# Attention followed by a channel mix on one core: order of the first loads, one transfer per piece in the first two batches, and a new order of all steps

## The chip, the cores and the metric

The kernel runs on one core of a Trainium2 chip, in one launch. The metric is device time in microseconds (us); the median of three timed runs is 259.61 us. Five engines work from queues of their own, each strictly in the order in which the program put its instructions: TensorE (PE; its weight loads are listed apart as PEld), VectorE (DVE), ScalarE (ACT), GpSimd (POOL) and SyncE (SP, which here only starts transfers). Transfers to and from the main memory (DMA) are started from the queues of SP, ACT and POOL. PE writes its products into PSUM, from where DVE and ACT fetch them.

## The reference, cut to what matters

Eight batches, eight heads, 576 tokens, 64 values per head. Attention is causal by blocks of 64 tokens; its output, with the heads side by side, is the input `x` of a channel mix with a token shift.

```
def _attn_ref(q, k, v):
    scores = scale * np.matmul(q, k.transpose(0, 1, 3, 2))
    scores = np.where(mask, scores, -1000000000.0)      # block_i >= block_j
    attn = np.exp(scores - np.max(scores, axis=-1, keepdims=True))
    attn = attn / (np.sum(attn, axis=-1, keepdims=True) + 1e-09)
    return np.matmul(attn, v)

def _moe_ref(x, mu_k, mu_r, w_k, w_v, w_r):              # x: 8 x 576 x 512
    x_prev = np.concatenate([zeros, x[:, :-1, :]], axis=1)
    xk = mu_k * x + (1.0 - mu_k) * x_prev
    xr = mu_r * x + (1.0 - mu_r) * x_prev
    k = np.maximum(xk @ w_k, 0.0)                        # 512 -> 1024
    v = k * k @ w_v                                      # 1024 -> 512
    r = 1.0 / (1.0 + np.exp(-(xr @ w_r)))                # 512 -> 512
    return r * v
```

## The kernel before

The work is written as 678 steps (`plan.add`), each with an engine and a function that issues its instructions. The table `ORDER` gives the order in which they are issued, by number; a number with `+n` issues n unread products first, which write the identity times itself into a PSUM buffer that is overwritten afterwards (`unread`, L222). The string `PLACE` picks the engine of each step that may run on more than one. Waits follow from the data and from the rings of buffers (`RINGS`): four buffers `nb` for loaded queries and keys, two `lv` for loaded values, four PSUM buffers `ps`, ten for exponentials `e`. A buffer is given to the step that comes next in the order, so the order sets the waits too.

**Attention of a batch b.** Queries and keys come in four pieces (`qkld b g n`: g the group of heads, n = 1 for keys, 0 for queries), loaded from POOL's queue (L249) with a cast from four-byte to two-byte numbers. DVE turns each piece (`turn`, L260) into the layout that PE multiplies. In the batches of `HALVES`, 0 and 1, a group g holds two heads of each half of the heads, so that the first half of the score steps needs only the two pieces with g = 0; there a piece consists of two stretches of memory, and before the change each is a transfer of its own, to 64 partitions. Values come from SP and, for batch 0, also from ACT (`vld`, L284); one engine casts them (`vc`, L214), and small copies on ACT (`hold`, L293) keep the values of batch 0 back until the first piece of keys is there. Scores are PE products of one 64-token block against others (`sc b unit`, L365); ACT takes their exponential (`ex`, L386). PE then forms the sums of the exponentials (`sum`, L524, or `av b S`, L449) and the weighted values (`av`, L544 or L460). DVE turns the sums, inverts them and multiplies (`t1`, `rec`, `t2`, `norm`). Batch 0 goes in two parts of 256 and 320 tokens, the others whole: `av b S`, `T`, `A` and `B`, of 60, 16, 72 and 72 products.

**Channel mix.** `d` (POOL, DVE or ACT) and `mul` (DVE, L600 or L604) make the mixed inputs `xk` and `xr`. Over nine chunks of 512 tokens, PE forms `pk` (key weights WK, L644), `pr` (WR, L687) and `pv` (WV, L721); ACT or DVE takes the positive part (`relu`), one of three engines the square (`sq`), ACT the tanh (L697), DVE the final product (`o`, L731), and SP stores (L740). The weights are ten transfers from POOL's queue (`wld`, L324): four for WK, two for WR, four for WV. The mixing factors are four small transfers from SP (`mus`, L756), from which DVE makes tables (`mu1`, L762 to L766).

In this order POOL's queue begins with the four pieces of batch 0, a cast of values, WK, WR and then the pieces of batch 1; PE goes from the attention of batch 0 to `pr 0 0` and `pk 0 0 0` and only then to the scores of batch 1. PE's queue has 8118 rows, half of them weight loads. In the trace and here, "row" of PE means one instruction.

Of the kernel before, what the change touches and what calls it, by code (L numbers as in the profile page):

```python
# [12 lines left out]
ALU = mybir.AluOpType  # L13

ORDER = """
# [35 lines left out]
"""  # L51

PLACE = (
    "DDDDPDPAPADDAPPAADAADPPDDPAPDPAAPPDADAPPPDAADAPDDAPDPDPDPAADPAAAADPAAA"
    "AAAAADPDADPAADPAPAPAPDDDAADAADPDAAPAAAPADAPADAADPADAA")


class Plan:
# [8 lines left out]
    def add(self, key, alts, fn, deps=(), uses=(), **info):  # L67
        t = {"key": key, "alts": alts, "eng": alts[0], "fn": fn,
             "deps": [d for d in deps if d is not None],
             "uses": list(uses), "fill": 0, "info": info}  # L70
        for b in t["uses"]:
            b["left"] += 1
        self.tasks.append(t)
        return t
# [37 lines left out]
def kernel(  # L112
# [12 lines left out]
    nc = tc.nc  # L125
    B, H, S, D = q.shape
    C = H * D
    DF = moe_w_k.shape[1]
    P = 128
# [3 lines left out]
    GH = 4  # L133
    QC = P // GH
    JT = S // D
    RW = 32
    TOK = S // RW
# [21 lines left out]
    LW = TOK * D  # L159
# [13 lines left out]
    def new(buf):  # L173

        return slots[buf["ring"], buf["slot"]]

    identb = consts.tile([P, P], BF)
# [21 lines left out]
    HALVES = (0, 1)  # L199
    add = plan.add  # L200
# [17 lines left out]
    def unread(t, dst):  # L218


        for _ in range(t["fill"]):
            nc.tensor.matmul(  # L222
                dst, identb,
                identb[:, :].unsqueeze(1).to_broadcast([P, 4, P]),
                start=True, stop=True)
# [9 lines left out]
    def add_qk(b, g, n):  # L235

        src, qkt = (q, k)[n], qkt_buf[b]
        nb = plan.buf("nb")  # L240

        def rows():
            return new(nb)

        def fetch(eng, me):
            parts = ([(D * y, D, GH * y + 2 * g, 2) for y in range(2)]
                     if b in HALVES else [(0, P, GH * g, GH)])
            for p0, np_, h0, nh in parts:
                nc.gpsimd.dma_start(  # L249
                    rows()[p0:p0 + np_],  # L250
                    src[b, h0:h0 + nh].rearrange(
                        "y (r j) d -> (y r) (j d)", j=TOK))
        t = add(f"qkld {b} {g} {n}", ("POOL",), fetch, uses=[nb], kind="ldc",
                kb=P * LW * 4 / 1024, starts=2 if b in HALVES else 1)

        if n:
            loads.setdefault(b, (nb, t))

        def turn(eng, me):
            nc.vector.transpose(  # L260
                new(qkt)[:, n, g].rearrange("p t e -> p (t e)").bitcast(
                    FP).rearrange("p (r j) -> p j r", r=RW),
                rows()[:, :].bitcast(FP).rearrange(
                    "p (j s) -> p j s", s=RW))
        evac["qkt", b, g, n] = add(f"turn {b} {g} {n}", ("DVE",), turn, [t],
                                   uses=[nb, qkt], kind="turn", cols=S)
# [436 lines left out]
    def add_pv(c, j0):  # L703
# [42 lines left out]

    wbuf = plan.buf("ps")

    add("spare", ("PE",), lambda eng, me: unread(me, new(wbuf)[:, 0]), uses=[wbuf],
        kind="spare", cols=[])  # L750
    mu_ready = []

# [18 lines left out]
    for b in range(B):  # L771
        for g in range(2):
            for n in range(2):
                add_qk(b, g, n)
        for m in range(2):
            add_v(b, m)
        if b == 0:
            for name, n in (("k", 4), ("r", 2), ("v", 4)):
                for i in range(n):
                    add_w(name, i)  # L780
            for p, (lo, hi) in enumerate(PARTS):
                add_part(b, p, [add_unit(b, f"{p}{i}", pieces, b in SPLIT)
                                for i, pieces in enumerate(PIECES[p])])
                for cc in range(CCn):
                    add_mix(b, cc, lo, hi,
                            [ready["x", b, x, cc % 2]
                             for x in range(max(p - 1, 0), p + 1)])
        else:
            add_av(b, [add_unit(b, f"{i}", pieces, b in SPLIT)
                       for i, pieces in enumerate(WHOLE)])  # L790
            for cc in range(CCn):
                add_mix(b, cc, 0, S, [ready["x", b, "AB"[cc % 2]],
                                      ready["x", b, "T"]])
# [40 lines left out]
```

## Time and profile before

| what | value |
|---|---|
| timed runs | 259.23, 259.61, 263.8 us; median 259.61 |
| the profiled execution: its time | 262.33 us |
| the profiled execution: its span | 260.2 us |
| DVE, ACT, POOL busy | 188.8, 162.4, 80.3 us |
| main memory read and written | 33.56 MB and 9.44 MB |
| unread products | 38 |

The span runs from the first to the last instruction; the execution's own time holds 2.1 us more around it. Busy shares are averages over stages with different limits. In the lists of groups and in the timeline a row ends with the idle time of the engine just before it and what ended it; "issue" there means that the engine waited for nothing that the profile shows. In the views by stretch, each engine's busy time stands with its number of instructions in brackets, then PE's granted clock (1.00 is full), the busy share of the DMA engines (it can exceed 1, since packets overlap) and what they moved.

### The profile page before, as it was taken

The numbers are of one execution on the slowest core, as the hardware profiler recorded it, in microseconds if no ns is written. First come the engines' busy times: TensorE is split into PE (matmuls) and PEld (weight loads), VectorE is DVE, ScalarE is ACT, GpSimd is POOL, SyncE is SP. The second block draws the span as 40 slices with busy tenths as digits, with TensorE's granted clock in tenths as the row PEclk, the third lists the DMA queues.
The fourth block names the chain that finished last, engine by engine and source line by source line (L and its number), as shares of the span: only waits on it lengthen the run. The fifth ranks groups of instructions, "written<-read, shape, count | busy, mean of one in ns | idle before, by whom it ended". The sixth has DMA issues, their size and how long they took to land.

```text
span 260.2 us, 8926 instructions
## 1 busy us (share of the span) xinstructions
PE 242.6 (93%) x4058; PEld 132.3 (51%) x4058; DVE 188.8 (73%) x233; ACT 162.4 (62%) x184; POOL 80.3 (31%) x88
## 2 busy tenths in 40 slices
PE   8859498879999999999999999999999999999994
PEld 3536356654454446644454487444554764444442
DVE  1737889597888699899688969884699389444322
ACT  1456048877656969796777786786887743274220
POOL 6074256841405610060455234420000221142000
PEclk9988989997999999999999999999999999999999
DMA  5999996899699995449785930021002200300224
GB/s 88 194 165 189 207 217 103 134 191 215 102 253 238 168 208 181 90 96 215 196 137 97 215 110 3 3 98 65 4 5 81 83 5 12 150 3 0 81 82 161
DMA packets 49189, 31.50 MB, mean 121 GB/s; under 512 B 38528, under 2 KB 39808, under 8 KB 49152
## 3 DMA queue, kind: packets, MB, share of 16 engines
q1 hardware_dynamic: 40128, 18.29, 29.7%
q0 software_dynamic: 6688, 12.06, 27.6%
q10 hardware_dynamic: 2336, 0.59, 1.5%
q8 instruction: 31, 0.51, 0.8%
q14 instruction: 6, 0.05, 0.1%
HBM read 33.56 MB, written 9.44 MB: 165 GB/s over the span
## 4 chain that ended last, share of the span: by engine, by line
PE 84%; DMA 6%; ACT 3%; issue 3%; DVE 1%; POOL 0%; ACTq 0%; DVEq 0%; POOLq 0%
PE t_ps L644 25%; PE t_ps L721 23%; PE t_ps L687 12%; PE t_ps L365 10%; PE t_ps L460 8%; PE t_ps L449 4%; DMA t_lv<-in_v_dram 4%; ACT t_e L386 2%; PE t_ps L544 2%; DMA t_nb<-in_k_dram 1%; DMA out_dram<-t_o 1%; PE t_ps L222 1%; DVE t_o L731 1%; PE t_ps L524 1%; ACT L293 0%
## 5 line engine op out<-in xcount | busy, mean ns | idle before, releaser
L386 ACT ACTIVATE t_e<-t_ps 128x1024 f16<-128x1024 f32 (+4 forms) x98 | 87.6, 957 | 30.9 <-PE t_ps L365 30.1
L644 PE MATMUL t_ps<-t_xk,WK 128*128 128x512 f16 (+3 forms) x416 | 66.9, 314 | 0.4 <-ACT t_e L386 0.3
L721 PE MATMUL t_ps<-WV,t_k 128*128 128x512 f16 (+1 forms) x296 | 64.6, 374 | 0.0
L671 POOL TENSOR_TENSOR t_k<-t_kr 128x1024 f16<-128x1024 f32 x16 | 30.5, 1907 | 76.9 <-DVE t_kr L661 62.5
L644 PEld LDWEIGHTS <-WK 128*128 128x128 f16 x416 | 37.0, 98 | 26.1 <-issue 2.4
L721 PEld LDWEIGHTS <-t_k 128*128 128x128 f16 x296 | 28.1, 98 | 33.1 <-issue 1.9
L365 PE MATMUL t_ps<-t_qkt 32*64 32x64 bf16 (+7 forms) x1344 | 37.3, 290 | 6.1 <-ACT t_e L386 3.8
L260 DVE STREAM_TRANSPOSE t_qkt<-t_nb 128x576 f32<-128x576 f32 x32 | 38.1, 1242 | 1.5 <-PE t_ps L365 1.0
L697 ACT ACTIVATE t_t<-t_ps 128x1024 f32<-128x1024 f32 x18 | 18.5, 1028 | 31.5 <-PE t_ps L687 31.5
L687 PE MATMUL t_ps<-WR,t_xr 128*128 128x512 f16 x144 | 35.1, 390 | 0.4 <-ACT t_e L386 0.4
L659 ACT ACTIVATE t_kr<-t_ps 128x1024 f32<-128x1024 f32 x22 | 22.4, 1024 | 18.8 <-PE t_ps L644 18.3
L365 PEld LDWEIGHTS <-t_qkt 32*64 32x64 bf16 x1344 | 21.8, 106 | 22.9 <-issue 17.9
L731 DVE SCALAR_TENSOR_TENSOR t_o<-t_t,t_ps 128x1024 f32<-128x1024 f32 (+2 forms) x20 | 22.1, 1108 | 14.9 <-PE t_ps L721 9.9
L661 DVE TENSOR_SCALAR t_kr<-t_ps 128x1024 f32<-128x1024 f32 x14 | 17.1, 1224 | 19.5 <-PE t_ps L644 19.4
L584 POOL TENSOR_TENSOR t_d<-t_xt 128x576 f32<-128x576 f32 (+2 forms) x10 | 11.6, 1162 | 36.3 <-DVE t_xk L604 13.5
L687 PEld LDWEIGHTS <-t_xr 128*128 128x128 f16 x144 | 13.7, 100 | 17.2 <-issue 2.5
L460 PE MATMUL t_ps<-t_e,t_vo 64*32 64x512 f16 (+7 forms) x1120 | 21.6, 295 | 0.0
L460 PEld LDWEIGHTS <-t_vo 64*32 64x32 f16 x1120 | 14.9, 95 | 8.8 <-issue 4.5
L604 DVE SCALAR_TENSOR_TENSOR t_xk<-t_d,MU,t_xt 128x576 f16<-128x576 f32 (+2 forms) x24 | 19.2, 802 | 0.1
L497 DVE TENSOR_TENSOR t_xt<-t_ps,t_rt 128x1024 f32<-128x1024 f32 x14 | 16.9, 1218 | 3.2 <-PE t_ps L460 3.1
L580 ACT ACTIVATE t_d<-t_xt,MU 128x576 f32<-128x576 f32 (+1 forms) x24 | 16.8, 751 | 3.7 <-DVE t_xr L604 2.6
L214 POOL CAST t_vo<-t_lv 128x1152 f16<-128x1152 f32 x8 | 9.7, 1216 | 30.5 <-PE t_ps L460 19.3
(40 smaller groups left out, 181.7 us busy)
## 6 DMA issues: line engine op xcount, KB each, us to landing
out_dram<-t_o SPq DMA_DIRECT2D x17, 512.0 KB, 3.3
t_lv<-in_v_dram SPq DMA_DIRECT2D x30, 288.0 KB, 6.3
t_nb<-in_k_dram POOLq DMA_DIRECT2D x12, 288.0 KB, 6.4
t_nb<-in_q_dram POOLq DMA_DIRECT2D x12, 288.0 KB, 6.2
t_nb<-in_k_dram POOLq DMA_DIRECT2D x8, 144.0 KB, 6.3
t_nb<-in_q_dram POOLq DMA_DIRECT2D x8, 144.0 KB, 6.3
WK<-in_moe_w_k_dram POOLq DMA_DIRECT2D x4, 256.0 KB, 6.7
WV<-in_moe_w_v_dram POOLq DMA_DIRECT2D x4, 256.0 KB, 9.0
```

The source lines that it names most:

```text
L260: nc.vector.transpose(new(qkt)[:, n, g].rearrange("p t e -> p (t e)").bitcast(FP).rearrange("p (r j) -> p j r", r=RW), rows()[:, :].bitcas ...
L365: nc.tensor.matmul(new(ms[a // 2])[y * D:y * D + D, a % 2, col:col + n], qkt[rows, 1, g, t * D:t * D + D, f], qkt[rows, 0, g, q0:q0 + n, f ...
L386: nc.scalar.activation(new(e)[:, 2 * h:2 * h + 2, 0:w], new(ms[h])[:, :, 0:w], AF.Exp, scale=ISQ)
L460: nc.tensor.matmul(PA[o, u, HALF + f * D:HALF + f * D + D] if kind == "T" else PA[o, u, lo - D:lo - D + n], weight(b, u, c, t % JT, f), E[ ...
L604: e.scalar_tensor_tensor(dst, dt[:, 0, 0:W], MU1[:, n, cc % 2, cc // 2:cc // 2 + 1], x, ALU.mult, ALU.add)
L644: nc.tensor.matmul(ps[:, x, y * w + a:y * w + a + n], WK[:, cc, jc * P:(jc + 1) * P], MIX[0][:, cc, at:at + n], start=(cc == 0), stop=(cc ...
L659: nc.scalar.activation(kt, ps, AF.Relu, scale=ROOT)
L671: (nc.vector if eng == "DVE" else nc.gpsimd).tensor_tensor(dst, KR, KR, ALU.mult)
L687: nc.tensor.matmul(ps[:, x], MIX[1][:, cc, g:g + P], WR[:, cc], start=(cc == 0), stop=(cc == CCn - 1))
L697: nc.scalar.activation(new(tb), new(m), AF.Tanh, scale=0.5)
L721: nc.tensor.matmul(ps[:, x, cols], k2[:, jc, at:at + P], WV[:, jc, cols], start=(jc == 0), stop=(jc == JCn - 1))
L731: nc.vector.scalar_tensor_tensor(new(o)[:, xs, cols], new(tb)[:, xs, cols], 1.0, new(m)[:, xs, cols], ALU.add, ALU.mult)
```

## The change

Four things change.

1. `fetch` in `add_qk`: in batches 0 and 1 a piece is now one transfer to 128 partitions whose source is two stretches of 64 rows (`y` in the rearrangement), instead of two transfers to 64 partitions. The bytes are the same.
2. The first step, `spare`, issues 25 unread products instead of 27, and in two goes; with the new order there are 32 in all instead of 38.
3. `PLACE` gives other engines to the steps that have a choice: 16 `d` on ACT instead of 12, 9 on DVE instead of 14; 24 `relu` on ACT instead of 22; the second cast of batch 0's values on POOL instead of DVE, among others.
4. `ORDER` is new throughout. On POOL the pieces of batch 1 come ahead of the weights; on PE most score steps of batch 1 come between the attention steps of batch 0, ahead of `pr 0 0` and `pk 0 0 0`; on SP the mixing factors go behind the values; at the end `pr 8 0` goes two steps ahead of `pv 7 2 0`.

```
 ORDER = """
-1 0+27 5 3 9 2 7 11 6 15 12 16 13 17 4 29 33 56 30 10 60 34 64 57 68 8 61 72
...
+5 0+25 3 9 7 15 6 11 12 16 13 17 1 4 29 33 10 56 30 60 34 64 57 68 8 61 72 65
...
         def fetch(eng, me):
-            parts = ([(D * y, D, GH * y + 2 * g, 2) for y in range(2)]
-                     if b in HALVES else [(0, P, GH * g, GH)])
-            for p0, np_, h0, nh in parts:
+            if b in HALVES:
                 nc.gpsimd.dma_start(
-                    rows()[p0:p0 + np_],
-                    src[b, h0:h0 + nh].rearrange(
+                    rows(),
+                    src[b].rearrange("(y g h) (r j) d -> g y h r (j d)",
+                                     y=2, g=2, j=TOK)[g])
+            else:
+                nc.gpsimd.dma_start(
+                    rows(), src[b, GH * g:GH * g + GH].rearrange(
                         "y (r j) d -> (y r) (j d)", j=TOK))
...
-    add("spare", ("PE",), lambda eng, me: unread(me, new(wbuf)[:, 0]), uses=[wbuf],
+    SHORT = 0
+
+    def spare(eng, me):
+        dst, rest = new(wbuf)[:, 0], me["fill"]
+        me["fill"] = min(rest, 10)
+        unread(me, dst)
+        for n in range(SHORT):
+            at = n % GH * RW
+            nc.tensor.matmul(dst[at:at + RW, 0:D], identb[:, 0:RW],
+                             identb[:, 0:D], start=True, stop=True)
+        me["fill"] = max(rest - 10, 0)
+        unread(me, dst)
+    add("spare", ("PE",), spare, uses=[wbuf],
```

The loop over `SHORT` runs zero times.

**DVE, at the start of the program.** Before, DVE's queue after the constants; MUT and MU are the tables of mixing factors, t_nb the loaded pieces, t_qkt the turned ones.

```order
L196 MEMSET t_xt_125 128x4
L762 STREAM_TRANSPOSE MUT<-MUS 128x64
L764 TENSOR_SCALAR MU_156<-MUT 128x4
L766 TENSOR_SCALAR MU_157<-MUT 128x4
L762 STREAM_TRANSPOSE MUT<-MUS 128x64
L764 TENSOR_SCALAR MU_156<-MUT 128x4
L766 TENSOR_SCALAR MU_157<-MUT 128x4
L260 STREAM_TRANSPOSE t_qkt_111<-t_nb_107 128x18x32
```

Now, the same place.

```order
L196 MEMSET t_xt_125 128x4
L262 STREAM_TRANSPOSE t_qkt_111<-t_nb_107 128x18x32
L262 STREAM_TRANSPOSE t_qkt_111<-t_nb_108 128x18x32
L262 STREAM_TRANSPOSE t_qkt_111<-t_nb_109 128x18x32
L262 STREAM_TRANSPOSE t_qkt_111<-t_nb_110 128x18x32
L776 STREAM_TRANSPOSE MUT<-MUS 128x64
```

The tables moved behind the four turns of batch 0.

**POOL, behind the pieces of batch 0.** Before; t_lv are loaded values, t_vo cast ones, t_d and t_xt belong to the mix.

```order
L249 DMA t_nb_110<-in_q_dram 64x1152 x2
L214 CAST t_vo_113<-t_lv_105 128x1152
L324 DMA WK<-in_moe_w_k_dram 128x1024 x4
L324 DMA WR<-in_moe_w_r_dram 128x1024 x2
L249 DMA t_nb_107<-in_k_dram 64x1152 x2
L584 ISA
L584 TENSOR_TENSOR t_d_131<-t_xt_125 128x256
L249 DMA t_nb_108<-in_q_dram 64x1152 x2
```

Now, from the last piece of batch 0 to the first of batch 2.

```order
L247 DMA t_nb_110<-in_q_dram 128x1x1152
L214 CAST t_vo_113<-t_lv_106 128x1152
L247 DMA t_nb_107<-in_k_dram 128x1x1152
L247 DMA t_nb_108<-in_q_dram 128x1x1152
L214 CAST t_vo_113<-t_lv_105 128x1152
L247 DMA t_nb_109<-in_k_dram 128x1x1152
L247 DMA t_nb_110<-in_q_dram 128x1x1152
L326 DMA WK<-in_moe_w_k_dram 128x1024 x3
L586 ISA
L586 TENSOR_TENSOR t_d_130<-t_xt_125 128x256
L326 DMA WK<-in_moe_w_k_dram 128x1024
L586 TENSOR_TENSOR t_d_131<-t_xt_125 128x256
```

The four pieces of batch 1 now come ahead of all weights, one row each; a second cast and two subtractions stand between the transfers, and `WR` and the pieces of batch 2 follow below.

**ACT, behind the exponentials of batch 0.** Before; t_e are exponentials (t_e_121 the last of batch 0, t_e_122 the first of batch 1), t_t the tanh.

```order
L386 ACTIVATE t_e_121<-t_ps_143 128x2x320
L697 ACTIVATE t_t_138<-t_ps_143 128x1024
L580 ACTIVATE t_d_130<-t_xt_125,MU_157 128x320 x2
L386 ACTIVATE t_e_122<-t_ps_145 128x1024
L386 ACTIVATE t_e_123<-t_ps_144 128x1024
```

Now, the same place.

```order
L388 ACTIVATE t_e_121<-t_ps_142 128x2x320
L388 ACTIVATE t_e_122<-t_ps_144 128x1024
L388 ACTIVATE t_e_123<-t_ps_145 128x1024
L388 ACTIVATE t_e_124<-t_ps_142 128x1024
L582 ACTIVATE t_d_130<-t_xt_125,MU_157 128x256 x2
L388 ACTIVATE t_e_115<-t_ps_145 128x1024
```

The exponentials of batch 1 now follow those of batch 0 directly; the first tanh comes after eight of them.

More of the change, by code (lines that the diff above doesn't have):

```diff
@@ L15 @@
 ORDER = """
[35 rows of a table removed]
[35 rows of a table added]
 """
 PLACE = (
-    "DDDDPDPAPADDAPPAADAADPPDDPAPDPAAPPDADAPPPDAADAPDDAPDPDPDPAADPAAAADPAAA"
-    "AAAAADPDADPAADPAPAPAPDDDAADAADPDAAPAAAPADAPADAADPADAA")
+    "PPPAADPPDDAPAAPDPADPAPADDAAPPPAAPPDDPADAAADAPAAADAAAAAAAPDADDAPAAAPAPD"
+    "AAPDAAPAPAPAADDDDAPAADDDPDPAAADDPAAAAAPAADPDDAPAAAPAD")
 class Plan:
@@ L245, in fetch @@
         def fetch(eng, me):
-            parts = ([(D * y, D, GH * y + 2 * g, 2) for y in range(2)]
-                     if b in HALVES else [(0, P, GH * g, GH)])
-            for p0, np_, h0, nh in parts:
+            if b in HALVES:
                 nc.gpsimd.dma_start(
-                    rows()[p0:p0 + np_],
-                    src[b, h0:h0 + nh].rearrange(
+                    rows(),
[4 more added lines that the diff above has]
+                    rows(), src[b, GH * g:GH * g + GH].rearrange(
                         "y (r j) d -> (y r) (j d)", j=TOK))
         t = add(f"qkld {b} {g} {n}", ("POOL",), fetch, uses=[nb], kind="ldc",
-                kb=P * LW * 4 / 1024, starts=2 if b in HALVES else 1)
+                kb=P * LW * 4 / 1024, starts=1)
         if n:
```

68 rows, old and new, of the table ORDER are left out of this document.

## The prediction

> **What bounds the kernel now.** I read the page first: the busy line, PE's slices, the DMA slices and the queues.
>
> ```profile
> span 260.2 us, 8926 instructions
> PE 242.6 (93%) x4058; PEld 132.3 (51%) x4058; DVE 188.8 (73%) x233; ACT 162.4 (62%) x184; POOL 80.3 (31%) x88
> PE   8859498879999999999999999999999999999994
> DMA  5999996899699995449785930021002200300224
> q8 instruction: 31, 0.51, 0.8%
> ```
>
> The reader is to see three things. PE is full from the tenth slice on, so the end is the moment at which PE becomes full, plus the work left then, plus a tail. DMA is full from the second slice to the fourteenth. And there is a queue that moves nothing of the kernel's: 31 packets, 0.51 MB, of instructions. PE's queue has 8118 rows; 8118/31 is 262 rows to a packet. So I looked at PE's timeline for places where it waits for nothing shown.
>
> ```profile
> 18.64 0.73 PE L544 MATMUL t_ps<-t_e,t_vo 64*32 64x256 f16 x30 [0.39 <-issue]
> 25.12 0.72 PEld L524 LDWEIGHTS <-pick 128*32 128x32 f16 x30 [0.42 <-issue]
> 25.92 1.60 PE L544 MATMUL t_ps<-t_e,t_vo 64*32 64x320 f16 x97
> 31.31 1.21 PE L544 MATMUL t_ps<-t_e,t_vo 64*32 64x320 f16 x63 [3.79 <-issue]
> 32.45 3.20 PE L687 MATMUL t_ps<-WR,t_xr 128*128 128x512 f16 x8
> 59.17 0.27 PE L365 MATMUL t_ps<-t_qkt 32*64 32x64 bf16 x3 [0.81 <-issue]
> ```
>
> The last stop but one is in the middle of one step: 97 products of it run, then 3.79 us of nothing, then the other 63, though all operands are there. Third, the stretches between such stops, and two where no transfers ran:
>
> ```profile
> 18.62:25.10 6.48, 6.39 (x128) 3.81 (x128) 5.58 (x12) 4.16 (x5) 2.90 (x6) 0.78 1.14 197
> 25.10:31.30 6.20, 2.40 (x128) 1.87 (x128) 5.00 (x11) 0.00 (x0) 2.31 (x5) 1.00 1.13 206
> 31.30:39.30 8.00, 7.76 (x125) 4.60 (x127) 6.60 (x8) 3.19 (x5) 3.68 (x6) 0.79 1.20 214
> 39.30:46.24 6.94, 5.96 (x133) 4.31 (x129) 6.76 (x10) 6.13 (x8) 4.79 (x5) 1.00 0.54 89
> 46.24:53.28 7.04, 6.60 (x137) 4.58 (x132) 4.30 (x6) 5.54 (x7) 5.83 (x8) 1.00 0.98 158
> 53.28:59.16 5.88, 3.94 (x130) 2.64 (x129) 5.81 (x8) 4.98 (x6) 1.78 (x3) 0.99 1.18 192
> 159.17:162.66 3.49, 3.49 (x145) 2.83 (x128) 3.05 (x6) 2.17 (x3) 0.18 (x2) 1.00 0.02 5
> ```
>
> From stop to stop stand 128 loads and 128 products: 256 rows. Call that a code page. With DMA full, a page takes 5.9 to 6.5 us even where its products need 2.40; with DMA empty, one passed in 3.49 us without a stop. So up to 31.3 us PE is bound by the arrival of its own code, which waits in a full DMA; from 31.3 to 53.3 by its work and by ACT; at 53.3 by code once more. After the long stop eight products took 3.20 us at a clock of 0.79.
>
> [...]
>
> **The change, part by part.**
>
> ```profile
> 6.80 0.24 DVE L762 STREAM_TRANSPOSE MUT<-MUS 128x64 f32<-128x64 f32 x1 [1.69 <-DMA MUS<-in_moe_mu_r_dram]
> 7.23 3.52 DVE L260 STREAM_TRANSPOSE t_qkt<-t_nb 128x576 f32<-128x576 f32 x3
> 9.61 2.59 PE L365 MATMUL t_ps<-t_qkt 32*64 32x256 bf16 x104 [0.95 <-DVE t_qkt L260]
> 5.32 1.28 ACT L293 ACT_TABLE_LOAD   x1 [5.32 <-DMA t_nb<-in_k_dram]
> 35.69 1.02 ACT L697 ACTIVATE t_t<-t_ps 128x1024 f32<-128x1024 f32 x1 [11.12 <-PE t_ps L687]
> 14.33 1.14 POOL L214 CAST t_vo<-t_lv 128x1152 f16<-128x1152 f32 x1 [8.76 <-ACT t_e L386]
> 28.56 0.52 POOL L249 DMA_DIRECT2D t_nb<-in_q_dram  x1 [1.00 <-DMA WR<-in_moe_w_r_dram]
> q0 software_dynamic: 640, 1.18, 85.0%
> ```
>
> *Start.* The first turn stood behind the mixing tables until 7.23, though its piece was there at 5.32, where ACT went on. Two turns of 3.52/3 = 1.17 us end at 7.7 if the queries are there by 6.5, and as before, at 9.6, if they come late. I take 8.3: 1.3 us earlier. The factors now go behind the values on SP; DVE has them back before its first sum at about 16, so nothing waits for them. Two unread products fewer cost nothing there, since PE waits for the turn.
>
> *Pages.* The stop at 18.64 belongs to a request made while the first scores ran, so it moves with them: 17.3. The new order then puts rows of the same kind behind it (exponentials' sums, score steps of batch 1, weighted values), and DMA is as full as before, since the pieces of batch 1 and WK only change places. Three pages of 6.3 us, the mean of 6.48 and 6.20: 23.6, 29.9, 36.2. The products in them (4.2, 3.0 and 2.5 us by counts of 32 score products of one step in 0.59, 60 sums in 1.36, 72 values in 1.32, all below) leave PE idle for half of it. Before, the same boundary was at 39.3: 3.1 gained. ACT's 11.12 us of idle time vanish; that gain is capped here.
>
> *The next pages.* Behind 36.2 come seven of batch 1's twelve exponentials, about 1 us each, with `pr 0 0`, `pk 0 0 0` and `pk 0 4 0` between and behind them: 7.2 us of products, and I allow 1.6 for PE and ACT waiting on each other. Then one page of 7.1: 45.0 and 52.1, against 53.28. Of the 3.1, 1.2 is left.
>
> *The last slow page* holds nothing but `av 1 A` and `av 1 B`, 2.35 us of products, with WV and the pieces of batch 3 in DMA: 5.9 like its like before. 58.0 against 59.16: **-1.2**. What is left behind it is three score steps of batch 2 (3 x 0.59) in place of one `av 1 B` (1.32): **+0.45**.
>
> ```profile
> 70.45 0.56 PE t_ps L365 x32
> 71.03 0.71 ACT t_e L386
> 78.99 0.14 issue
> 88.12 1.24 DVE t_xt L497
> 207.35 1.36 PE t_ps L449 x60
> 211.96 1.32 PE t_ps L460 x72
> 215.11 6.91 PE t_ps L721 x32
> 252.47 1.23 DVE t_o L731
> 253.72 2.80 DMA out_dram<-t_o
> 256.64 0.42 DVE t_o L731
> ```
>
> *Weights.* WK and WR now stand behind four whole pieces. Two weights' landings ended POOL's waits, the last at 28.56 with six weights issued from 14.33 + 1.14 = 15.5 on: 2.2 us each with the values beside them. Four pieces of 288 KB where a weight has 256 take some 9.7 us: WR at 38, where I have `pr 0 0` at 37. Between 0 and 1.3: **+0.4**. The second cast of values on POOL costs 1.14 us ahead of two pieces; these are turned only behind the 29.9 boundary, which covers it. Four transfers fewer per batch save POOL 0.52 us each, while it has waited 8.76 us anyway: nothing.
>
> *Stalls on the way* (the chain's rows above): 0.71, 0.14 and 1.24 us between 71 and 90. I see other waits of the kind in the new order but no reason that all stay: **-1.0** (0 to -2.1). *New dense pages:* two more pages, in batches 4 and 5, hold only `av A`, `T` and `B`, 2.35 us; no page before passed in under 3.49. Each costs 0 to 1.1 with DMA empty, up to 3.9 with DMA full; slices there are mostly under half: **+1.3**. *End:* the third-last `o` starts when the store 253.72 + 2.80 has landed; with `tanh 8 0` earlier it doesn't wait: **-0.4**.
>
> Sum: -1.2 + 0.45 + 0.4 - 1.0 + 1.3 - 0.4 = -0.45. Against the profiled execution's 262.33 us that is 261.9; the median is 259.61, 2.7 lower, so **259.2**. Its own range is 254.5 to 264: pages at their ends, dense pages full or free.
>
> **The rivals.**
>
> *The merged transfer runs on few DMA engines.* Its source is two stretches of 64 rows; every transfer of POOL's in the trace has 64 or 128 rows outermost. No row shows how the 16 engines share one with two. If by rows, nothing changes. If by the outermost two, two engines carry 64 rows each. In the window from 2 to 11 us the software queue (last row quoted in the second-last fence) has 1.18 MB, 512 rows of 2304 bytes, in 85% of 16 engines' 9 us: 0.24 us a row at most, 0.19 if the tiny packets are taken out at equal weight (640). So 12 to 15 us a piece instead of 1.5 to 1.9. The keys of batch 0 come 11 to 13 later, the first product 9 to 11, and with them the values, which are held back for the keys. Batch 1's pieces are issued behind the first cast, now at 15.5 + 11, and take 12 to 15 and a landing: 40 to 43 instead of 22 (two of 2.4 behind 15.5, and a landing), so its scores start at 42 to 45 instead of 24; the two code waits in between (some 5 us) fall away. +12 to +15.5: **271 to 275, say 272**, slower. It decides from about 6 us a piece upward. For it speaks the shape alone; against it only that nothing like it has been seen.
>
> [...]
>
> *Code stops binding.* If pages came in 3.5 us, as with DMA empty, 36.2 would be 33.8 (ACT's pace), the last slow page 2.4 shorter, the dense pages free, and the half clock behind the stops gone (8 products took 3.20 where 32 take 6.91, so 1.5): -2.4 - 2.4 - 1.3 - 1.5 = -7.6, **251.6**, or 253.5 with half the clock and the start kept. Against it: 1.13 to 1.20 of DMA in every page of the front, and the bytes don't change.
>
> *Batch 1's loads gain nothing*, because POOL's casts hold them back: then the front stays as before, 260 to 262, within 2%.
>
> **How the numbers follow.** Main sum with its near variants (the third rival among them) 0.45; few engines 0.37; code stops binding 0.13; other losses, such as every dense page at full DMA and new waits, over 264.8: 0.05. The predicted time is the likeliest's, 259.2; the 8-in-10 range must reach into the few-engines case: 254 to 274. Two per cent, 5.2 us, is about what a measurement of this kernel can tell from no change. Faster by more (under 254.4): 0.15, all from the code case and the main sum's edge. Slower by more: 0.37 + 0.05 = 0.42. Within: 0.43.
>
> **What would show it.** Landing of batch 0's first keys at 5 to 6 us, or at 16 to 19: that decides first. First score product at 8.3. Stops marked "issue" with 128 loads between them, near 17.3, 23.6, 29.9 and 36.2; a stop inside `av 1 B` ending near 58. ACT without a gap of 11 us. The last `o` rows without a wait for a store. I am wrong if PE is full well before 58 us with DMA still full, or if there are no such stops.

## The result and the profile after

| kernel | time, median | ratio to before, 95% interval |
|---|---|---|
| before (six runs) | 260.14 us | |
| changed (six runs) | 282.26 us | 1.087 [1.080, 1.093] |

Medians here and below are of all runs; ratios leave out runs more than 1.5% above their kernel's fastest, among them one of 1326.48 us in the first experiment. The change makes the kernel slower by 22.1 us. The prediction gave 259.2 us as the likeliest time and 254 to 274 as the range; the time lies above the range. The case named first among the rivals, a merged transfer on few DMA engines, is what happened, and its price of 272 was still 10 us short.

The page of the changed kernel, in the order in which that of before was read (busy line, PE, its granted clock and DMA in 40 slices, the software queue):

```profile
span 280.4 us, 8900 instructions
PE 242.9 (87%) x4052; PEld 133.4 (48%) x4052; DVE 186.9 (67%) x227; ACT 169.3 (60%) x194; POOL 79.0 (28%) x80
PE   8238507799598999798999899999999999999995
PEclk9859955999979999999999999999999999999999
DMA  3589979689955999896691992002100400210124
q0 software_dynamic: 13728, 12.09, 27.3%
```

PE is busy as long as before (242.9 us against 242.6), so the 20.2 us of span are idle time. They lie in the first twelve slices: PE falls to 2, 3 and 0, at 7 to 21 us and at 35 to 42 us. The software queue (q0, POOL's transfers) moves the same bytes in twice the packets; on the page of before it stands as

```profile
q0 software_dynamic: 6688, 12.06, 27.6%
```

The chain of work that ended last names what was waited for (start, duration, what):

```profile
1.25 14.73 DMA t_nb<-in_k_dram
...
16.32 6.44 DMA t_lv<-in_v_dram
...
24.00 16.46 DMA t_nb<-in_k_dram
```

The first keys of batch 0 take 14.73 us, the values held back for them follow, and then the first keys of batch 1 take 16.46 us. PE's timeline of the changed kernel shows the two waits, and a stop inside `av 1 B` (in the changed kernel's line numbers L367 is `sc`, L462 `av`, L723 `pv`):

```profile
18.46 4.92 PE L367 MATMUL t_ps<-t_qkt 32*64 32x256 bf16 x128 [9.83 <-DVE t_qkt L262]
44.00 2.77 PE L367 MATMUL t_ps<-t_qkt 32*64 32x512 bf16 x32 [10.95 <-DVE t_qkt L262]
75.61 0.21 PE L462 MATMUL t_ps<-t_e,t_vo 64*32 64x64 f16 x5 [3.46 <-issue]
```

The first score product comes at 18.46 instead of 9.61, and batch 1's scores at 44.00. Ahead of them PE waits 9.83 and 10.95 us for DVE's turns, which wait for the pieces. How many DMA engines work meanwhile is in the stretches: of the changed kernel from 8 to 15 us, where nothing but the four pieces of batch 0 is under way, and of the kernel before from 3 to 9.5 us. The last three numbers of a row are PE's clock, the DMA share and GB/s.

```profile
8.00:15.00 7.00, 0.63 (x3) 0.10 (x1) 0.00 (x0) 0.00 (x0) 0.00 (x0) 0.79 0.55 103
```

```profile
3.00:9.50 6.50, 5.66 (x23) 2.33 (x22) 3.14 (x9) 1.57 (x3) 2.57 (x5) 1.00 1.01 160
```

A share of 0.55 is 8.8 of 16 engines for four pieces, about two for each; before, the share is 1.01. Whether the two stretches of the source do that, and what the rest of the change does, needs experiments.

### The profile page after: what moved, and what is told of

The parts are those of the page before. It is cut to its first block, busy times and chain, and to the rows that moved or that the text cites. A ratio compares the mean times of both kernels' runs of the same rounds, so it can differ in the third digit from the quotient of the medians.

```text
span 280.4 us, 8900 instructions
## 1 busy us (share of the span) xinstructions
PE 242.9 (87%) x4052; PEld 133.4 (48%) x4052; DVE 186.9 (67%) x227; ACT 169.3 (60%) x194; POOL 79.0 (28%) x80
## 3 DMA queue, kind: packets, MB, share of 16 engines
q0 software_dynamic: 13728, 12.09, 27.3%
## 4 chain that ended last, share of the span: by engine, by line
PE 76%; DMA 13%; issue 5%; ACT 3%; DVE 2%; POOLq 0%; DVEq 0%; POOL 0%; ACTq 0%
PE t_ps L723 23%; PE t_ps L646 23%; DMA t_nb<-in_k_dram 11%; PE t_ps L689 11%; PE t_ps L367 8%; PE t_ps L462 7%; PE t_ps L451 3%; ACT t_e L388 2%; DMA t_lv<-in_v_dram 2%; DVE t_qkt L262 1%; PE t_ps L546 1%; DVE t_xt L558 1%; DVE t_d L586 0%; ACT t_t L699 0%; DVE t_o L733 0%
## 5 line engine op out<-in xcount | busy, mean ns | idle before, releaser
L723 PE MATMUL t_ps<-WV,t_k 128*128 128x512 f16 (+1 forms) x296 | 66.6, 380 | 0.0
L367 PE MATMUL t_ps<-t_qkt 32*64 32x64 bf16 (+7 forms) x1344 | 38.8, 298 | 25.1 <-DVE t_qkt L262 21.7
L723 PEld LDWEIGHTS <-t_k 128*128 128x128 f16 x296 | 28.5, 99 | 34.6 <-issue 4.5
L367 PEld LDWEIGHTS <-t_qkt 32*64 32x64 bf16 x1344 | 23.3, 110 | 43.0 <-issue 19.8
L661 ACT ACTIVATE t_kr<-t_ps 128x1024 f32<-128x1024 f32 x24 | 24.7, 1027 | 15.3 <-PE t_ps L646 15.2
L689 PE MATMUL t_ps<-WR,t_xr 128*128 128x512 f16 x144 | 33.8, 379 | 0.1
L663 DVE TENSOR_SCALAR t_kr<-t_ps 128x1024 f32<-128x1024 f32 x12 | 14.7, 1224 | 17.4 <-PE t_ps L646 17.4
L462 PE MATMUL t_ps<-t_e,t_vo 64*32 64x64 f16 (+7 forms) x1120 | 20.7, 284 | 4.4 <-issue 4.3
L582 ACT ACTIVATE t_d<-t_xt,MU 128x576 f32<-128x576 f32 (+1 forms) x32 | 21.9, 737 | 2.0 <-DVE t_xr L602 0.7
L462 PEld LDWEIGHTS <-t_vo 64*32 64x32 f16 x1120 | 15.3, 92 | 12.3 <-issue 9.1
L689 PEld LDWEIGHTS <-t_xr 128*128 128x128 f16 x144 | 13.6, 98 | 15.5 <-issue 0.2
L671 ACT ACTIVATE t_k<-t_kr 128x1024 f16<-128x1024 f32 x13 | 13.7, 1057 | 6.6 <-DVE t_kr L663 6.3
L606 DVE SCALAR_TENSOR_TENSOR t_xk<-t_d,MU,t_xt 128x576 f16<-128x576 f32 (+2 forms) x20 | 16.3, 818 | 0.0
```

What stands on the lines that cost most here:

```text
L367: nc.tensor.matmul(new(ms[a // 2])[y * D:y * D + D, a % 2, col:col + n], qkt[rows, 1, g, t * D:t * D + D, f], qkt[rows, 0, g, q0:q0 + n, f ...
L462: nc.tensor.matmul(PA[o, u, HALF + f * D:HALF + f * D + D] if kind == "T" else PA[o, u, lo - D:lo - D + n], weight(b, u, c, t % JT, f), E[ ...
L582: nc.scalar.activation(dt[:, n, 0:W], x[:, cc, lo0:hi], AF.Copy, scale=MU2[:, n, cc % 2, cc // 2:cc // 2 + 1])
L661: nc.scalar.activation(kt, ps, AF.Relu, scale=ROOT)
L689: nc.tensor.matmul(ps[:, x], MIX[1][:, cc, g:g + P], WR[:, cc], start=(cc == 0), stop=(cc == CCn - 1))
L723: nc.tensor.matmul(ps[:, x, cols], k2[:, jc, at:at + P], WV[:, jc, cols], start=(jc == 0), stop=(jc == JCn - 1))
```

## The experiments

Times are medians; the kernel before ran beside each group: 260.71 us in the first, 260.93 in the second, 261.68 in the third.

### Two transfers again

The changed kernel with the merge alone undone; order, places and unread products stay.

```
             if b in HALVES:
-                nc.gpsimd.dma_start(
-                    rows(),
-                    src[b].rearrange("(y g h) (r j) d -> g y h r (j d)",
-                                     y=2, g=2, j=TOK)[g])
+                for y in range(2):
+                    nc.gpsimd.dma_start(
+                        rows()[D * y:D * y + D],
+                        src[b, GH * y + 2 * g:GH * y + 2 * g + 2].rearrange(
+                            "y (r j) d -> (y r) (j d)", j=TOK))
```

> The changed kernel with one thing undone: in batches 0 and 1 a piece is two transfers to 64 partitions again; order, places and unread products stay changed. Few-engines theory (a transfer whose source has two stretches outermost runs on two DMA engines): the first keys land at 5 to 6 us instead of 15.98, the first score product is at 8 to 9.6, batch 1's pieces land by 30, and the time is the main sum of the prediction, 259.2, within 254.5 to 264. Rival, the new order is at fault: the loads come early, PE still waits about 10 us for batch 1's turns, and the time stays above 270.

Measured: 267.56 us, 1.022 [1.017, 1.027]. Neither theory had it: the merge costs some 15 us, but the rest of the change costs 7 as well. The trace of this run is of the execution of 1326.48 us, for which no reason is known, so the same kernel was run again:

> The changed kernel with two transfers to a piece again in batches 0 and 1, a second time beside the runs of this call, for a trace of its own. 265.5 to 269, and PE's stops where the kernel with the 64 rows outermost has them: near 17.6, 25.4, 31.6, 38.1 and 62.3 us.

Measured: 267.94 us, 1.027 [1.020, 1.034]. Of the five stops expected, none shows near 17.6, three are in place, and the last ends at 59.96 instead of 62.3. Its PE timeline, at the places that matter (L368 `sc`, L527 `sum`, L547 and L463 `av`, L690 `pr`, L724 `pv`, L647 `pk`; the bracket is the idle time ahead of the row):

```profile
9.24 2.60 PE L368 MATMUL t_ps<-t_qkt 32*64 32x256 bf16 x104 [0.61 <-DVE t_qkt L263]
...
25.14 0.60 PE L527 MATMUL t_ps<-t_e,pick 128*32 128x320 f16 x24 [2.96 <-issue]
...
31.34 0.24 PE L547 MATMUL t_ps<-t_e,t_vo 64*32 64x128 f16 x9 [1.20 <-issue]
...
35.07 0.64 PE L368 MATMUL t_ps<-t_qkt 32*64 32x512 bf16 x7 [1.32 <-DVE t_qkt L263]
37.53 1.29 PE L368 MATMUL t_ps<-t_qkt 32*64 32x512 bf16 x25 [1.82 <-issue]
38.75 1.90 PE L690 MATMUL t_ps<-WR,t_xr 128*128 128x512 f16 x8
...
52.96 2.68 PE L463 MATMUL t_ps<-t_e,t_vo 64*32 64x64 f16 x155
59.96 0.24 PE L463 MATMUL t_ps<-t_e,t_vo 64*32 64x64 f16 x5 [4.32 <-issue]
...
61.15 4.64 PE L724 MATMUL t_ps<-WV,t_k 128*128 128x512 f16 x16
...
66.30 3.63 PE L724 MATMUL t_ps<-WV,t_k 128*128 128x512 f16 x16
```

The long waits for pieces are gone. Left are stops for nothing shown, the long one with 155 products of `av` ahead of it and 5 of `av 1 B` behind. The prediction took such stops for waits for code, and the trace agrees: during the 4.32 us of the long one the instruction queue moves one packet of 0.02 MB, and ahead of the end of each of the four stops such a packet lands, by 1.3 to 1.7 us. Behind the long stop 16 products of `pv` take 4.64 us where the next 16 take 3.63: the granted clock is 0.78 in the first stretch and 1.00 in the second.

### Only the merge, in the kernel before

The same merge put into the kernel before, nothing else.

> The kernel before with one thing of the change: in batches 0 and 1 a piece is one transfer to 128 partitions from two stretches of memory; order, places and unread products are those of before. Few-engines theory: the four pieces of batch 0 land at 16 to 19.3 us and those of batch 1 take 12 to 17 us each from issue to landing; the first score product comes 8.9 later, some 5 us of waits for code fall away, so 266 to 275. Rival, the order is at fault: within 2% of before, 255 to 265.

Measured: 277.48 us, 1.064 [1.059, 1.069], so 16.8 us, a little over the range. Its chain has both groups of pieces:

```profile
2.26 15.26 DMA t_nb<-in_q_dram
...
32.96 20.89 DMA t_nb<-in_q_dram
```

Batch 1's pieces take 20.89 us, not the 12 to 17 expected. In this order weights and values move beside them: during these 20.89 us the software queue moves 2.00 MB, of which the four pieces are 1.18, and the values' queue 0.70 MB. That this is what slows them is argued, not shown. The merge alone costs 14.3 us in the new order (282.26 less 267.94) and 16.8 in the old one.

### One transfer, other outermost sizes

Is it that there is a single transfer, or that the outermost size of its source is two? Two kernels keep one transfer of the same bytes and change the view of the source. The first has the 64 rows outermost, the second four stretches of 32 rows.

```
-                    src[b].rearrange("(y g h) (r j) d -> g y h r (j d)",
-                                     y=2, g=2, j=TOK)[g])
+                    src[b].rearrange("(y g h) (r j) d -> g (h r) y (j d)",
+                                     y=2, g=2, j=TOK)[g])
```

```
+                    src[b].rearrange("(a g) (r j) d -> g a r (j d)",
+                                     g=2, j=TOK)[g])
```

> The changed kernel, still one transfer to a piece and the same bytes, but with the 64 rows outermost in the source and the two stretches inside them, so that the rows of a piece lie in another order on the partitions (the scores of batches 0 and 1 are then of mixed heads). Few-engines theory, by the outermost size: 64 rows spread over 16 engines, each piece lands 2 to 4 us after its issue, and the time equals that of the same kernel with two transfers to a piece within 1%. Rival, one transfer from two stretches is slow in itself (its descriptors or its one completion): 12 to 15 us a piece and 278 to 285.

> The changed kernel, still one transfer to a piece and the same bytes, but from four stretches of 32 rows (every second head) instead of two of 64; the scores of batches 0 and 1 are then of other pairs of heads. Few-engines theory, by the outermost size: four engines with 32 rows each, 32 x 0.19 to 0.21 = 6.1 to 6.7 us and 2.4 of start and landing, so batch 0's first keys at 9.8 to 10.5 us and the first product at about 12.5; 262 to 268. Rival, stretches don't matter, only that it is one transfer: 14.7 us a piece and 278 to 285.

Measured: 269.21 us for 64 (1.027 [1.019, 1.034]), within 1% of the kernel with two transfers; 271.91 for four (1.039 [1.035, 1.044]), above its range, which stood on the main sum of the prediction and so lacked the 7 us of the order; its first product came at 13.80, not at 12.5. DVE's first turn starts when the first keys have landed; with 64, four and two outermost, one row of each kernel's DVE timeline:

```profile
5.35 2.64 DVE L262 STREAM_TRANSPOSE t_qkt<-t_nb 128x576 f32<-128x576 f32 x2 [3.88 <-DMA t_nb<-in_k_dram]
```

```profile
10.75 1.26 DVE L262 STREAM_TRANSPOSE t_qkt<-t_nb 128x576 f32<-128x576 f32 x1 [9.29 <-DMA t_nb<-in_k_dram]
```

```profile
16.01 4.69 DVE L262 STREAM_TRANSPOSE t_qkt<-t_nb 128x576 f32<-128x576 f32 x4 [14.55 <-DMA t_nb<-in_k_dram]
```

Going from four to two outermost adds 5.26 us. If the outermost size is the number of engines, each engine gets 32 more rows of 2304 bytes, and at the 0.192 us that one mostly takes in the trace they are 6.1. The software queue's packets on the pages of 64 and of four count the same thing:

```profile
q0 software_dynamic: 6560, 12.06, 27.1%
```

```profile
q0 software_dynamic: 9632, 12.07, 27.4%
```

Against 64 outermost, four has 3072 more packets, 384 to each of eight pieces, which is 12 x 32; two has 13728 - 6560 = 7168 more, 896 to a piece, which is 14 x 64. They have four bytes each: 7168 of them add 0.03 MB to the queue (12.09 against 12.06). Each engine that carries no row seems to get one such packet for each row of an engine that does; this is read from the counts alone. So four and two outermost go with four and two engines, by landings and packets; with 64 the DMA share from 3 to 9.5 us is 1.02, as with two transfers to a piece (1.01). Other sizes were not tried.

### Merged in one batch

The merge in batch 1 alone, then in batch 0 alone.

> The changed kernel with one transfer to a piece in batch 1 alone; batch 0's pieces are two transfers each. Few-engines theory: the start is that of the kernel with two transfers (first product near 9.1), batch 1's pieces are issued at 15 to 19 us and take 13 to 17, so they land at 30 to 34 instead of 18 to 26; its first scores start at 32 to 35 instead of 26.3, and the stops for code before 38 us cover a part: 2 to 6 us above the kernel with two transfers. Rival, only batch 0's transfers matter since nothing hides them: within 1 us of it.

> The changed kernel with one transfer to a piece in batch 0 alone; batch 1's pieces are two transfers each. Few-engines theory: first product at 18.5 instead of 9.1, and about 5 us of stops for code fall away behind it: 4 to 8 us above the kernel with two transfers. If both batches' costs simply added up, the two kernels with one merged batch would lose 14.7 us together, 282.3 less 267.6.

Measured: 273.6 us (1.049 [1.044, 1.054]) and 275.06 us (1.055 [1.051, 1.058]): 5.7 and 7.1 above the kernel with two transfers, both in their ranges. PE's row of batch 1's first scores in the one (later than the 32 to 35 expected), and of the first product in the other:

```profile
36.11 2.77 PE L373 MATMUL t_ps<-t_qkt 32*64 32x512 bf16 x32 [13.25 <-DVE t_qkt L268]
```

```profile
18.47 5.47 PE L373 MATMUL t_ps<-t_qkt 32*64 32x256 bf16 x144 [9.53 <-DVE t_qkt L268]
```

Together they cost 12.8 of the merge's 14.3. In the first, the packets of code of the stops that ended at 25.14 and 31.34 land at 19.7 and 27.8 us, before PE needs them; these two stops are gone, and the later ones shrink from 1.82 and 4.32 us to 1.08 and 3.52. In the second the four stops are about as long as without the merge (2.32, 1.25, 1.82 and 4.51 us), and its trace is 9.3 us longer, as much as its first product is late. That the medians lie only 7.1 apart is within what the four runs of the kernel with two transfers differ (265.95 to 269.53).

### The rows shifted

Left is the order's 7 us. Counted in the program, with a load and a product for each, the four stops stand at rows 702, 958, 1214 and 1982 of PE's queue, multiples of 256 apart; the stops of the kernel before at 31.31 and 59.17 stand at 958 and 1982 too, in other steps. If the stop in `av 1 B` belongs to the row's number, short products ahead of everything move it elsewhere. To the kernel with two transfers:

```
-5 0+25 3 9 7 15 6 11 12 16 13 17 1 4 29 33 10 56 30 60 34 64 57 68 8 61 72 65
+5 0+14 3 9 7 15 6 11 12 16 13 17 1 4 29 33 10 56 30 60 34 64 57 68 8 61 72 65
...
-    SHORT = 0
+    SHORT = 72
```

> The changed kernel with two transfers to a piece, and with 14 unread products at the start instead of 25 and 72 short ones (64 columns) among them, so that the rest of PE's queue stands 122 rows further on. Code-page theory (stops belong to a row's number in the queue, one every 256 rows, not to a step): the stop of 3.4 us inside av 1 B near 62 us shrinks to under 1 and the 16 products of pv behind it take 3.6 us instead of 5.7; in the front the boundaries fall into other steps and one half page more is waited for, which costs about 3: 262 to 268 in all. Rival, the stop belongs to what av 1 B reads (values or exponentials late in a way the profile doesn't name): the stop of over 3 us stays inside av 1 B.

Measured: 258.1 us, 0.988 [0.985, 0.992], ten runs: 9.8 below the same work unshifted, and 1.2% below the kernel before, which is clear of the noise but less than the two per cent that the prediction took as telling. It is below the expected 262 to 268, since the half page in the front cost nothing. PE's timeline (L760 are the short products):

```profile
4.61 0.76 PE L760 MATMUL t_ps<-identb 128*32 128x64 bf16 x72
...
9.05 2.59 PE L368 MATMUL t_ps<-t_qkt 32*64 32x256 bf16 x104 [2.72 <-DVE t_qkt L263]
...
33.44 0.79 PE L547 MATMUL t_ps<-t_e,t_vo 64*32 64x320 f16 x54 [3.25 <-issue]
...
51.50 3.00 PE L463 MATMUL t_ps<-t_e,t_vo 64*32 64x64 f16 x160
...
55.02 3.63 PE L724 MATMUL t_ps<-WV,t_k 128*128 128x512 f16 x16
```

The 160 products run through, and `pv` runs at full clock (1.00 granted). From the start of `av 1` to the start of the first `pv` pass 3.52 us (51.50 to 55.02) instead of 8.19 (52.96 to 61.15), and that `pv` takes 1.0 less: 5.7. `av 1` begins 1.5 earlier, though more rows lie ahead of it: the 144 short rows (72 products and their loads) took 0.76 us of a time in which PE waits for data anyway, 2.72 us of it still idle. The spans differ by 9.2 us (264.2 and 255.0); the rest, about 2, comes later, with a stop of 0.45 us in `av` and 1.5 us from a stretch at half clock that the unshifted kernel had.

Three controls and a cross-check went together. One shifts by a whole page (`SHORT = 139`), one has the 14 products and none of the short, one shifts the changed kernel, merged transfers and all, and one the kernel before (with 16 unread products where it had 27, and the 72 short ones).

> The changed kernel with two transfers to a piece, 14 unread products and 139 short ones: the rest of PE's queue stands 256 rows further on than with 25 and none, one whole page. Code-page theory: the boundary falls on the same product of av 1 B as without the shift (155 before the stop, 5 behind it), and the stop of 3 to 4.5 us and the half clock behind it are back; 264 to 269, the time of the kernel without the shift. Rival, the short products help by themselves (clock kept up, code asked for earlier, fewer large ones): no stop there and 256 to 260, as with 72 of them.

> The changed kernel with two transfers to a piece and 14 unread products, none of the short ones: the queue stands 22 rows earlier than with 25. Code-page theory: av 1 A and B still lie in one page of 2.5 us of products, so the stop of 3 to 4.5 us comes right behind av 1 B, in the first score step of batch 2; 264 to 269. Rival, the gain came from taking eleven large products away: 256 to 260.

> The changed kernel itself, merged transfers and all, with 14 unread products and 72 short ones (122 rows on). Code-page theory: the stop of 3.46 us at 75.6 and what follows it go, the front, which waits for data, is covered: 272 to 277 instead of 282.3. If the merge is all that was wrong: 280 to 284.

> The kernel before, order and transfers untouched, with 16 unread products at the start instead of 27 and 72 short ones (122 rows on). Code-page theory: in this place av 1 A, two short score steps and av 1 B share a page of 2.65 us of products, and batch 2's av another of 2.81, so stops of 2 to 4 us appear inside av 1 B and av 2 B, and the front waits for half a page more: 264 to 271. Rival, short products help by themselves: 256 to 260.

Measured: 265.97 (1.015 [1.009, 1.022]), 266.85 (1.012 [1.005, 1.018]), 273.53 (1.046 [1.039, 1.053]) and 269.43 us (1.031 [1.025, 1.038]), all four in the ranges of the code pages. In the changed kernel, shifted, the stop in `av 1 B` is gone too and the `pv` behind it takes 3.63 us. PE's rows: shifted by 256,

```profile
54.53 2.68 PE L463 MATMUL t_ps<-t_e,t_vo 64*32 64x64 f16 x155
61.42 0.21 PE L463 MATMUL t_ps<-t_e,t_vo 64*32 64x64 f16 x5 [4.21 <-issue]
...
62.16 5.31 PE L724 MATMUL t_ps<-WV,t_k 128*128 128x512 f16 x16
```

with fourteen alone,

```profile
52.26 2.71 PE L463 MATMUL t_ps<-t_e,t_vo 64*32 64x64 f16 x160
54.90 0.42 PE L368 MATMUL t_ps<-t_qkt 32*64 32x512 bf16 x6
58.67 1.06 PE L368 MATMUL t_ps<-t_qkt 32*64 32x512 bf16 x10 [3.35 <-issue]
```

the kernel before, shifted,

```profile
64.02 0.22 PE L460 MATMUL t_ps<-t_e,t_vo 64*32 64x64 f16 x8 [1.92 <-issue]
...
64.76 3.63 PE L721 MATMUL t_ps<-WV,t_k 128*128 128x512 f16 x16
...
79.14 1.23 PE L460 MATMUL t_ps<-t_e,t_vo 64*32 64x384 f16 x44 [2.29 <-issue]
80.30 3.06 PE L644 MATMUL t_ps<-t_xk,WK 128*128 128x512 f16 x8
```

and unshifted, the same products, each step in one row with no stop in it:

```profile
59.36 2.55 PE L460 MATMUL t_ps<-t_e,t_vo 64*32 64x512 f16 x72
...
73.74 1.47 PE L460 MATMUL t_ps<-t_e,t_vo 64*32 64x64 f16 x88
```

A page further, the stop is back between the same two products, 155 and 5. Twenty-two rows earlier it is eleven products further on, in the first score step of batch 2. The kernel before gets stops inside `av 1 B` and `av 2 B` that it did not have. So a part of its 260 us hangs on where its rows lie: the same shift costs the kernel before 7.8 us and saves the new order 9.8, or 7.9 if measured against the shift by a whole page.

Put together: the new order with its rows well placed is 2.8 us faster than before (258.1 against 260.93); with its rows as written it loses 9.8; the merge loses another 14.3. That these add up to about the 22.1 measured is no test, since each figure is the difference between one kernel and the next, from 260.93 to 282.26. The test is that the merge costs much the same wherever the rows lie: 15.4 with the rows shifted (273.53 less 258.1), 14.3 without.

## Why the prediction was wrong

Two steps failed: the choice of the likeliest case, and the base from which the case that came true was priced.

*The choice of the likeliest case.* "If by rows, nothing changes. If by the outermost two, two engines carry 64 rows each": the prediction gave the first 0.45 and the second 0.37, and the second is shown. Its details came out close: 12 to 15 us a piece (14.73 for the first), keys at 16 to 19 (16.0), first product 9 to 11 later (8.85), batch 1's scores at 42 to 45 (44.00), +12 to +15.5 for the whole (14.3 in this order). That batch 1's scores came in time is partly luck: its keys were issued at 24.00, not at 26.5, and took 16.46 us, not 12 to 15. What failed was the weight, and the reason given for it, that all other transfers have 64 or 128 rows outermost: that said that nothing like it had been seen, not that it would be harmless.

*The base under that rival.* 272 was worked out from the kernel before, as if the new order were worth nothing beside the merge. The order as written costs 7, where the sum of the prediction had -0.45, and 272 + 7 would have been near the 282.

*Start, -1.3.* Measured -0.4 (9.24 against 9.61, two transfers): the second turn waited for the queries, as the sentence on late queries allowed. That nothing waits for the factors is wrong too: in the shifted kernel the transfers of MUS, which now stand behind the values, are in the chain for 4.72 us, and PE waits 1.73 us for a turn of sums that stands behind the tables on DVE.

*Pages of the front: 17.3, 23.6, 29.9, 36.2.* Stops of this kind came: none shows at 17.3, but three end at 25.14, 31.34 and 37.53. When the code of a page is asked for, no trace shows; the request during the first scores was an estimate. The later pages took 6.20 and 6.19 where 6.3 was taken, so the lateness, 1.3 to 1.5, is from ahead of the first of the three. ACT's gap of 11.12 us went as foretold: its longest up to 45 us is 5.94.

*The last slow page, 58.0, -1.2.* The stop is where it was foretold, inside `av 1 B`, but ends at 59.96, 0.8 after its like before (59.17). Of the 2.0 us missing, about 1.3 came from the front, and the rest lies here.

*Behind it.* From that boundary to the end before had 201.0 us (260.2 - 59.17), the kernel with two transfers 204.2 (264.2 - 59.96): +3.2, where the terms 0.45, -1.0, +1.3 and -0.4 make +0.35. The most mis-sized term is "stalls on the way, -1.0", and the lower clock behind stops has no term. PE's later timeline of that kernel:

```profile
71.24 0.66 PE L368 MATMUL t_ps<-t_qkt 32*64 32x384 bf16 x30 [0.57 <-DVE t_o L734]
...
98.36 0.73 PE L368 MATMUL t_ps<-t_qkt 32*64 32x320 bf16 x32 [0.60 <-DVE t_o L734]
99.70 0.49 PE L368 MATMUL t_ps<-t_qkt 32*64 32x256 bf16 x30 [0.61 <-ACT t_e L389]
100.62 3.46 PE L647 MATMUL t_ps<-t_xk,WK 128*128 128x128 f16 x16 [0.43 <-ACT t_e L389]
...
141.72 0.33 PE L463 MATMUL t_ps<-t_e,t_vo 64*32 64x192 f16 x17 [0.45 <-issue]
```

The old waits went and 2.2 us of others came (0.57 + 0.60 + 0.61 + 0.43), so idle time on the way grew by about 1.0 instead of falling by 1.0. The dense pages of batches 4 and 5, +1.3, showed one stop of 0.45 in this trace: within their ends, and less than was taken. PE's busy time behind the boundary is 2.3 us longer than before (198.3 against 196.0); +0.45 was forecast for the work, and the rest, about 1.8, is clock. (The kernel before has such a stretch too: its `av 1 B` takes 2.55 us, where 72 such products take 1.39 elsewhere.) Part of it is the `pv` of 4.64 us behind the long stop. Another is the `pk` at 100.62: it takes 3.46 us at a granted clock of 0.52, where the same 16 products take 1.91 in the shifted kernel, below. Shifted by 256, with the pages as unshifted, they take 1.91 as well, so this stretch does not come from where the rows lie, and its cause stays open.

```profile
93.69 1.91 PE L647 MATMUL t_ps<-t_xk,WK 128*128 128x128 f16 x16 [0.43 <-ACT t_e L389]
```

*Weights, +0.4.* Nothing: `pr 0 0` follows on at 38.75 without a wait for WR.

*End, -0.4.* Right in kind: in the changed kernel's chain the last `o` comes straight behind PE, and no store stands in it.

```profile
273.83 3.49 PE t_ps L723 x24
277.31 0.02 issue
277.34 0.42 DVE t_o L733
```

*Readings of the trace before.* Of the stretches quoted, one, not two, has no transfers (a share of 0.02), and the clock of 0.79 is that of the 8 us from 31.30; in the 3.2 us of the eight products it was 0.58. Neither enters the sum.

*The other rivals.* "Code stops binding" did not happen: stops stay in every kernel tried, the longest of each between 2.29 and 4.64 us, but move. The third, that POOL's casts hold back batch 1's loads, was not tried by itself; with two transfers PE's longest wait for a turn behind the start is the 1.32 us at 35.07.

## What to carry to other kernels

Ahead of merging transfers, look at the outermost size of the source: here 64, four and two, with the same bytes and as many transfers, had DVE's first turn start at 5.35, 10.75 and 16.01 us, so bytes and count did not tell how many engines worked. The DMA share did: 0.55 while DVE waited for the first keys, where before it was 1.01. In these kernels, with some 8100 rows in PE's queue (4052 products and as many loads), row numbers were part of the schedule, since 122 rows were worth 9.8 us: compare two orders only with their page boundaries looked at, and try a shift by half a page before judging an order. A rival's price is to be added to what the rest of the change does, not to the kernel before.

## What the hardware showed that was not expected

A shift of PE's rows by 122, with 72 short products whose results nobody reads, put where PE waits anyway, changed the time by 9.8 us of 268, and by 7.8 us the other way in the kernel before. With fourteen alone, a page of 2.5 us of products (122 of the 160 of `av`, which took 2.71, and six of a score step in 0.42) ended in a stop of 3.35 us; inside `av 1 B`, in the other kernels with the new order that stopped there, it was 3.38 to 4.64. With two transfers to a piece, pages of the front followed each other by 6.2 us, with DMA slices there at 7 to 9 tenths. That a page's code takes these 6.2 us to come here too, which would make the stop 3.7, is the author's estimate. A stop can also cost behind its end: after one of 4.21 us, the next 16 products of `pv` took 5.31 us at a granted clock of 0.68, with full clock 3.63. In the kernel before, shifted, `pv` took 3.63 behind a stop of 1.92 us, and behind one of 2.29 eight products of `pk` took 3.06, where eight take 1.89 a little later. From how long a stop on it happens, and whether the length alone decides, was not tried.
